# Gated mix of memory attention and GEGLU on one core: repeated waits on TensorE, and the last output part in partition halves

## The chip, the cores and the metric

The kernel runs on one core of a Trainium2 chip. The metric is the device time of one execution in microseconds, the median of three runs. One further execution is taken with the hardware profiler; every duration below that has a row is from that one execution.

## The reference

```python
x = A_x                                            # (1, 2048, 512) bf16
g = sigmoid((x * gate_w).sum(-1, keepdims=True))   # one gate per token
a = A_ref(x, wq, wk, wv, wo, beta)                 # attention with a memory
b = B_ref(x, w_gate, w_up, w_down)                 # (gelu(x@w_gate) * (x@w_up)) @ w_down, inner width 1792
return g * a + (1 - g) * b
```

`A_ref` splits the 2048 tokens into 4 segments of 512 and has 32 heads of width 16. In each segment it takes a causal softmax attention inside the segment, and adds, weighted by `sigmoid(beta)`, a read of a memory `M, z` that the earlier segments have built from `phi(k)` and `v`, with `phi(t) = t + 1` for positive `t` and `exp(t)` else. Then `M` and `z` take up the segment's own keys and values, and the joined heads go through `wo`.

## The kernel before

**The work of one segment.** Keys, queries and values are dense products (`K`, `Q`, `V`: four TensorE products of 128x512 each into one PSUM bank), each evicted by ScalarE or VectorE. The scores are "fills" (`st`): eight row-tiled products that fill the four banks of `psX`; ScalarE takes the exponential of all 2048 columns at once (`exp`, line 661) into `pt`, and GpSimd multiplies the causal triangles in (`msk`, line 667). There are 18 fills in a segment, 72 in all, and as there is only one `psX` a fill has to wait until the exponential of the fill before has been read out. `pv` (line 698) multiplies with the values: 64 small products in one go, four times a segment. VectorE transposes and normalizes (`tp`, `pvp`, `ot`). `mz` and `nd` write and read the memory. The GEGLU part has 14 gate products (`G`), 14 up products (`U`, one after the other `Us_fta` and `Us_ftb` of two TensorE products each, both into the same bank, line 487), 14 multiplications on VectorE (`h`, line 824), and the down products `out` (line 837). Behind them stand the output projection `wo` (line 854), the eviction of the down product with the factor 1-g (`wev`, lines 842 and 845), the sum of the two on VectorE (`oev`, line 858) and the store (`dma`, line 863).

**What sets the order.** The program is a list of tasks with reads and writes. `ORDER`, a text at the end of the file, names all of them in the order in which they are issued; a digit behind a colon is the PSUM bank or buffer taken, an `a` or `d` says whether ScalarE or VectorE does an eviction. Each engine gets its own tasks in this order. `Emitter.finalize` works out which semaphore values each instruction has to wait for, leaving out those that the engine has already waited for, and `Emitter.emit` (line 237) puts a `wait_ge` for each ahead of the instruction. The last of these waits rides on the instruction itself. Further ones become wait instructions of their own; in the trace they are `EVENT_SEMAPHORE` at line 241.

**The end of the program.** The fast program takes the exponentials without subtracting a row maximum. A test (`chk`, `okrow`, `oksum`, `flag`, lines 727 to 738) finds out whether that was safe for the data. Every engine loads the flag into a register (`reg_*`, `TENSOR_LOAD`, line 742), and compares and branches (line 961): when all is well it jumps to the end, past a second, general program of that engine that subtracts the maxima. That program is long: on VectorE 1024 of its instructions are the row maxima (two for each of 512, lines 770 to 774), on TensorE the fills have a second product for each of theirs. Near the start of its stream each engine executes a hint that names this branch (line 951; `HINT` says behind how many instructions). Behind the branch all engines drain and meet (line 971). SyncE, and only SyncE, waits for the stores: for the early ones ahead of its last three tasks, for two of them ahead of its branch, and for the last three behind it (line 992).

**The last two row blocks.** Token blocks 14 and 15 (128 tokens each) have their output projection and the sum in two column halves of 256, to shorten the last steps. Block 14 is stored as a whole from SyncE. Block 15 is stored in two parts: columns 0 to 255 from SyncE, columns 256 to 511 from ScalarE.

## Time and profile before

| | |
|---|---|
| median of 3 runs | 267.12 us (267.05 to 267.35) |
| the profiled execution's own time | 268.07 us |
| its span, first to last instruction | 266.3 us |
| around the span | 268.07 - 266.3 = 1.77 us |
| granted TensorE clock | 0.997 |
| TensorE busy | 254.0 us |
| VectorE, ScalarE, GpSimd busy | 214.5, 209.6, 96.6 us |

PE is the TensorE matmul, PEld its weight load, DVE VectorE, ACT ScalarE, POOL GpSimd, SP SyncE; a `q` behind the name (PEldq, SPq) marks an instruction of that engine's sequencer: waits, register loads, branches, drains and the issue of DMAs. `L487` is line 487 of the kernel. In a list of instructions by source line the columns are the engine, the operation, the count, the shortest, median and longest duration in ns, and the first and last start in us. In a list by time they are start, duration, engine, line, operation, and in brackets the idle time before with what ended it. The end of a TensorE product is modelled, about 380 ns for 128x512, while the next one can start 216 ns after it.

### The profile page before, as it was taken

The numbers are of one execution on the slowest core, as the hardware profiler recorded it, in microseconds if no ns is written. First come the engines' busy times: TensorE is split into PE (matmuls) and PEld (weight loads), VectorE is DVE, ScalarE is ACT, GpSimd is POOL, SyncE is SP. The second block draws the span as 40 slices with busy tenths as digits, with TensorE's granted clock in tenths as the row PEclk, the third lists the DMA queues.
The fourth block names the chain that finished last, engine by engine and source line by source line (L and its number), as shares of the span: only waits on it lengthen the run. The fifth ranks groups of instructions, "written<-read, shape, count | busy, mean of one in ns | idle before, by whom it ended". The sixth has DMA issues, their size and how long they took to land.

```text
span 266.3 us, 6561 instructions
## 1 busy us (share of the span) xinstructions
PE 254.0 (95%) x2729; PEld 112.4 (42%) x2766; DVE 214.5 (81%) x421; ACT 209.6 (79%) x174; POOL 96.6 (36%) x159
## 2 busy tenths in 40 slices
PE   7999999999999999999999999999999999999991
PEld 4634434444344444444434344334444443434450
DVE  0676776689999797999798989998988986959872
ACT  2578999989899999999988879568889976577420
POOL 6024332065551526160452644433407217263400
PEclk9999999999999999999999999999999999999998
DMA  6897179802547203002021001000110000000011
GB/s 205 237 177 234 39 108 192 245 23 62 158 62 100 61 20 109 12 0 63 0 64 42 20 2 62 2 21 2 43 35 7 0 2 21 21 22 1 22 39 47
DMA packets 26624, 17.19 MB, mean 65 GB/s; under 512 B 14302, under 2 KB 26078, under 8 KB 26590
## 3 DMA queue, kind: packets, MB, share of 16 engines
q1 hardware_dynamic: 26014, 16.27, 25.3%
q10 hardware_dynamic: 576, 0.46, 0.6%
q8 instruction: 22, 0.36, 0.6%
q14 instruction: 12, 0.10, 0.1%
HBM read 10.36 MB, written 2.10 MB: 47 GB/s over the span
## 4 chain that ended last, share of the span: by engine, by line
PE 93%; issue 2%; DMA 2%; DVE 1%; SPq 0%
PE psD L487 51%; PE psD L837 18%; PE psX L645 9%; PE psD L698 6%; PE psD L854 5%; DMA pt<-in_A_x_dram 2%; PE psD L582 1%; PE psD L515 1%; PE psX L600 0%; PE psD L509 0%; DVE ost L858 0%; SPq L357 0%; PE psD L588 0%; PE psX L908 0%; DVE kD L526 0%
## 5 line engine op out<-in xcount | busy, mean ns | idle before, releaser
L661 ACT ACTIVATE pt<-psX 128x2048 bf16<-128x2048 f32 x72 | 135.1, 1877 | 28.6 <-PE psX L645 27.4
L667 POOL TENSOR_TENSOR pt<-pt,ctri 128x256 bf16<-128x256 bf16 x128 | 91.2, 719 | 151.8 <-ACT pt L661 147.3
L487 PE MATMUL psD<-xT,wu 128*128 128x512 bf16 x214 | 54.1, 380 | 1.4 <-issue 1.3
L837 PE MATMUL psD<-wd,gb 128*128 128x512 bf16 x217 | 54.1, 380 | 0.9 <-issue 0.8
L487 PE MATMUL psD<-xT,wg 128*128 128x512 bf16 x217 | 54.1, 380 | 0.9 <-issue 0.8
L824 DVE TENSOR_TENSOR gb<-psD,gb 128x512 bf16<-128x512 f32 x56 | 37.3, 684 | 8.6 <-PE psD L487 8.3
L837 PEld LDWEIGHTS psD<-wd,gb 128*128 128x128 bf16 x224 | 20.5, 98 | 26.1 <-issue 2.8
L487 PEld LDWEIGHTS psD<-xT,wu 128*128 128x128 bf16 x224 | 20.3, 98 | 26.1 <-issue 2.8
L487 PEld LDWEIGHTS psD<-xT,wg 128*128 128x128 bf16 x224 | 20.1, 98 | 26.4 <-issue 3.2
L557 DVE STREAM_TRANSPOSE tT<-psD 128x512 f32<-128x512 f32 x35 | 24.1, 703 | 7.7 <-PE psD L698 5.8
L645 PE MATMUL psX<-qT,kD 32*128 32x192 bf16 (+7 forms) x512 | 28.5, 287 | 0.0
L645 PEld LDWEIGHTS psX<-qT,kD 32*128 32x128 bf16 x512 | 8.2, 92 | 25.2 <-ACT pt L661 20.9
L698 PE MATMUL psD<-pt,vnat 64*17 64x128 bf16 (+7 forms) x512 | 18.8, 283 | 0.0
L698 PE MATMUL psD<-pt,vsh 64*17 64x128 bf16 (+7 forms) x512 | 18.3, 283 | 0.0
L710 DVE SCALAR_TENSOR_TENSOR ob<-tT,gq,rcall 128x256 bf16<-128x256 f32 x32 | 16.6, 517 | 1.1
L487 PE MATMUL psD<-wv,xT 128*128 128x512 bf16 x61 | 16.8, 380 | 0.4 <-issue 0.3
L487 PE MATMUL psD<-xT,wq 128*128 128x512 bf16 x59 | 16.2, 379 | 0.7 <-issue 0.5
L480 DVE CAST gb<-psD 128x512 bf16<-128x512 f32 x19 | 12.9, 686 | 3.9 <-PE psD L487 3.9
L854 PE MATMUL psD<-wo,oT 128*128 128x512 bf16 (+1 forms) x69 | 15.5, 354 | 0.5 <-issue 0.5
L698 PEld LDWEIGHTS psD<-pt,vnat 64*17 64x17 bf16 x512 | 11.6, 86 | 8.9 <-POOL pt L667 4.2
L815 ACT ACTIVATE gb<-psD 128x512 bf16<-128x512 f32 x28 | 14.8, 603 | 0.6 <-PE psD L487 0.5
L842 ACT ACTIVATE wds<-psD,omgt 128x512 f32<-128x512 f32 x8 | 5.5, 686 | 12.1 <-PE psD L837 7.4
(99 smaller groups left out, 275.8 us busy)
## 6 DMA issues: line engine op xcount, KB each, us to landing
xg<-in_A_x_dram SPq DMA_DIRECT2D x16, 128.0 KB, 2.2
out_dram<-ost SPq DMA_DIRECT2D x15, 128.0 KB, 1.7
wg<-in_B_w_gate_dram SPq DMA_DIRECT2D x2, 896.0 KB, 6.8
wu<-in_B_w_up_dram SPq DMA_DIRECT2D x2, 896.0 KB, 5.9
wd<-in_B_w_down_dram SPq DMA_DIRECT2D x2, 896.0 KB, 6.7
vsh<-vnat SPq DMA_DIRECT2D x16, 68.0 KB, 2.1
wq<-in_A_wq_dram SPq DMA_DIRECT2D x2, 256.0 KB, 5.3
wv<-in_A_wv_dram SPq DMA_DIRECT2D x1, 512.0 KB, 3.9
```

What stands on the lines that cost most here:

```text
L480: (DVE, 0.60, [I(lambda e: e.tensor_copy(dst, src()), [bk(sl), *reads], writes)]),
L487: one(f"{name}{'abcd'[h // 2]}", PE, 2 * T_MM, [I(lambda e, i=i: e.matmul(BK[sl.i][:, :], lhs(i), rhs(i), start=(i == 0), stop=(i == n - 1 ...
L557: one(f"tp{name}", DVE, 0.605, [I(lambda e, ts=ts, bank=bank: e.transpose(tT[ts.i][:, :], bank()), [key], [("tT", ts)])])
L645: ins.append(I(lambda e, c=c, kb=kb, ncol=ncol, c0=c0, g=g: e.matmul(XALL[:, g * 512 + c0:g * 512 + c0 + ncol], kD[b][quad(g), c, kb, :], ...
L661: one(f"exp{s}_{name}", ACT, 2048 * 0.000833 + 0.05, [I(lambda e: e.activation(pt[slot][:, :, :], xin, ACTF.Exp, scale=ATT_SCALE), [("X", ...
L667: ins.append(I(lambda e, mv=mv: e.tensor_tensor(mv, mv, cm, ALU.mult), [("pt", slot), ("causal",)], [("pt", slot)]))
L698: ins.append(I(lambda e, kb=kb, slot=slot, c0=c0, n=n, g=g, c=c, r0=r0, sl=banks[j], va=va: e.matmul(BK[sl.i][32 * c:32 * c + 17, 64 * kb: ...
L710: I(lambda e, ts=ts, t=t, j=j, dst=dst, r=r: e.scalar_tensor_tensor(out=dst, in0=t_rows(ts, 16), scalar=gq[:, 2 * t + j:2 * t + j + 1], in ...
L815: one(f"gd{s}_{ft}", ACT, 0.485, [I(lambda e, gi=gi, f=f, sl=sl: e.activation(gb[gi][:, f, :], BK[sl.i][:, :], ACTF.Gelu_apprx_tanh), [bk( ...
L824: one(f"h{s}_{ft}", DVE, 0.605, [I(lambda e, sl=sl, gi=gi, f=f: e.tensor_tensor(gb[gi][:, f, :], BK[sl.i][:, :], gb[gi][:, f, :], ALU.mult ...
L837: mm.append(I(lambda e, fb=fb, gi=gi, f=f, q=q, sl=sl: e.matmul(BK[sl.i][:, :], gb[gi][:, f, q], wd[:, fb, :], start=(fb == 0), stop=(fb = ...
L854: one(f"wo{s}_{qt}_{ci}", PE, 4 * T_MM / len(parts), [I(lambda e, kb=kb, q=q, so=so, c=c: e.matmul(BK[so.i][:, c], oT[:, kb, q], wo[:, kb, ...
```

## The change

Three edits go together. The first makes `emit` put the last wait that the engine had met a further `again` times ahead of an instruction, and sets `again = 2` for the last instruction of every `U` task: the second and the fourth product of each of the 56 up products, 112 instructions on TensorE. Each of them then has two more waits, both for a value that has been reached.

The second changes the stores of block 15. Columns 0 to 255 go out from ScalarE. Columns 256 to 511 go out in two DMAs, partitions 0 to 63 from SyncE and 64 to 127 from ScalarE. The lists of stores that SyncE waits for move by one.

The third is a new `ORDER`: the same tasks, and the one new store, in another order, with some evictions given to the other engine and other banks.

```diff
         self.inc = False
+        self.again = 0
...
         self.order = []
+        self.met = {}
...
             for sem, val in spec.waits:
                 e.wait_ge(sem, val)
+                self.met[eng] = sem, val
+            for _ in range(spec.again):
+                e.wait_ge(*self.met[eng])
             ins = spec.fn(e)
...
-                        one(f"dma{gt}_{ci}", (SP, ACT)[last and ci], 0.5, [I(lambda e, gt=gt, oi=oi, d=d: e.dma_start(
-                            out[0, gt * 128:(gt + 1) * 128, d], ost[oi][:, d]), kd, [("out", gt, ci)],
-                            dma_sem=sem(f"s_out{gt}_{ci}"))], lat=2.0)
-                        outs.append(f"s_out{gt}_{ci}")
+                        rows = ((ci, SP if not last else ACT, 0, P),) if not (last and ci) else ((1, SP, 0, 64), (2, ACT, 64, P))
+                        for n, eng, lo, hi in rows:
+                            one(f"dma{gt}_{n}", eng, 0.5, [I(lambda e, gt=gt, oi=oi, d=d, lo=lo, hi=hi: e.dma_start(
+                                out[0, gt * 128 + lo:gt * 128 + hi, d], ost[oi][lo:hi, d]), kd, [("out", gt, n)],
+                                dma_sem=sem(f"s_out{gt}_{n}"))], lat=2.0)
+                            outs.append(f"s_out{gt}_{n}")
...
+    for t, eng, instrs in order:
+        if t.name[0] == "U":
+            instrs[-1].again = 2
     em.finalize()
...
-            for name in outs[:-5]:
+            for name in outs[:-6]:
...
-            for name in outs[-5:-3]:
+            for name in outs[-6:-4]:
...
-            for name in outs[-3:]:
+            for name in outs[-4:]:
...
 ORDER = """
-ld_x0_0 wake0:0 ld_x0_1 ld_wk0 ident wake1 ld_wk1 xtr0_00 ld_x0_2 xtr0_01 ld_x0_3 ld_wk2 ld_wq0 xev0_00:a xev0_01:a
...
-wo3_0_0:3 wev3_1:a wo3_1_0:0 oev3_0_0 dma11_0 oev3_1_0 out3_3_2 out3_3_3 chk3 out3_3_4 dma12_0 okrow wev3_2:a
-wo3_2_0:2 wev3_3:a wo3_2_1:3 oev3_2_0 wo3_3_0:0 wo3_3_1:1 oev3_2_1 dma13_0 oev3_3_0 oev3_3_1 oksum:2 dma14_1 dma15_0
-flag dma15_1 reg_pe reg_act reg_dve reg_pool reg_sp
+ld_x0_0 causal1 wake0:0 ident ld_x0_1 ld_wk0 wake1 ld_wk1 xtr0_00 ld_x0_2 xtr0_01 ld_x0_3 ld_wk2 xtr0_03 xev0_00:a
+xev0_01:d xev0_03:d ld_wq0 xtr0_02 ld_wq1 xev0_02:d K0_k0:1032 ld_wv K0_k1 xtr0_11 xtr0_10 ld_beta ld_wg0 xtr0_12
...
+G1_3a:2 mzm0 G1_3b G1_4a:3 Gev1_2:a gs4 msk0_3D gs5 st1_0A:0 G1_4b exp1_0A phkb1_2 msk1_0A U0_12a:1 Gev1_3:d ld_xg6
+ld_xg7 U0_12b Kev2_1:d Gev1_4:d h0_12 pv0_3:20 st1_0B:0 tp0_d30:1 pvp0_30 ld_wd1 out0_1_0:1 ld_x3_3 pvp0_21 out0_1_1
+tp0_d31:2 out0_1_2 exp1_0B K2_3a:2 st1_0D:0 phqb1_0 phkc1_2 K2_3b out0_1_3 K2_2a:0 Q2_3a:3 gs6 exp1_0D K2_2b ktr1_0
+Kev2_3:a Q2_3b ktr1_1 Kev2_2:a vsh1_01 ot0_2 msk1_0B Qev2_3:a st1_0E:0 phqc1_2 ktr1_2 msk1_0D K2_0a:2 V2_3a:0 V2_3b
+Vev2_3:d exp1_0E K2_0b out0_0_0:3 st1_0C:0 Kev2_0:a out0_0_1 pvp0_31 exp1_0C kpada2_3 vsh1_00 ld_wo20 out0_3_0:0 gs7
...
+ot3_3 wo3_0_0:0 wo3_1_0:3 oev3_0_0 oev3_1_0 chk3 out3_3_2 out3_3_3 dma12_0 out3_3_4 okrow wev3_2:a dma13_0 wo3_2_0:3
+oev3_2_0 wo3_2_1:0 wo3_3_0:2 oev3_2_1 wev3_3:a wo3_3_1:3 oksum:1 oev3_3_0 oev3_3_1 flag dma14_1 dma15_0 dma15_1
+dma15_2 reg_pe reg_act reg_dve reg_pool reg_sp
```

Counted in the two texts: TensorE has 524 tasks in both, and 78 stretches of row-tiled work (fills, `pv`, `mz`, `nd` and the first transposes) between dense products in both. In both, exactly ten dense products of 128x512 lie between one fill and the next in 33 places. The first 16 DMAs that SyncE issues are the same in the same order. The last five tasks of TensorE, and the last five of VectorE, come in the same order in both.

## Prediction

> **What bounds the kernel now.** I read the page first, then TensorE's waits, then the last microseconds line by line.

> ```profile
> span 266.3 us, 6561 instructions
> ...
> PE 254.0 (95%) x2729; PEld 112.4 (42%) x2766; DVE 214.5 (81%) x421; ACT 209.6 (79%) x174; POOL 96.6 (36%) x159
> ```

> TensorE is busy for 95% of the span. That its products also follow each other without holes is in a stretch of the timeline, which I chose because a wait instruction stands in it (below):

> ```profile
> 47.97 1.89 PE L487 MATMUL psD<-xT,wg 128*128 128x512 bf16 x8
> 49.70 1.03 PE L487 MATMUL psD<-xT,wq 128*128 128x512 bf16 x4
> 50.56 0.81 PE L487 MATMUL psD<-xT,wu 128*128 128x512 bf16 x3
> ```

> From 47.97 to 50.56 twelve products start in 2.59 us, 0.216 us each. The list of TensorE's own waits has nothing longer than 0.8 us, and its largest entry is small:

> ```profile
> PE psD L487 <- issue: 3.2, 20, 0.2
> PE psX L399 <- PEq L1112: 0.8, 1, 0.8
> ```

> So until about 260 us the time is the number of products and of changes between dense and row-tiled work, and another order can save there only by having fewer. Then comes the end. The chain of waits for the last 16 us runs over TensorE, the last sums and the flag, and stops at 261.01; the span stops at 266.3. What lies between are sequencer instructions, seen by listing the branch line and the drain line:

> ```profile
> 260.04 0.92 DVE ost L858 x2
> 260.96 0.05 DVE flag L738
> ```

> ```profile
> L961 POOLq COMPARE_BRANCH  x1: 65/65/65, 261.6 to 261.6; - x1
> L961 PEldq COMPARE_BRANCH  x1: 4322/4322/4322, 261.6 to 261.6; - x1
> L961 SPq COMPARE_BRANCH  x1: 83/83/83, 261.6 to 261.6; - x1
> L961 DVEq COMPARE_BRANCH  x1: 84/84/84, 261.8 to 261.8; - x1
> L961 ACTq COMPARE_BRANCH  x1: 68/68/68, 261.9 to 261.9; - x1
> ```

> ```profile
> L971 SPq DRAIN  x1: 13/13/13, 262.9 to 262.9; - x1
> L971 PEldq DRAIN  x1: 63/63/63, 266.0 to 266.0; - x1
> ```

> ```profile
> L992 SPq EVENT_SEMAPHORE  x1: 27/27/27, 262.6 to 262.6; - x1
> ```

> **This is the fact on which I build:** five engines take the same branch, four need 65 to 84 ns, TensorE 4322. Its drain stands at 266.0, the next latest, SyncE's behind the last store, at 262.9. TensorE's branch alone holds the kernel open for the last 3.1 us, and the stores are hidden behind it.

> **The change part by part.**

> *The waits.* 56 up products have two halves each: 112 instructions get two waits. As before, one rides on the instruction and one stands alone, so TensorE's stream is 112 instructions longer. What a standing wait costs:

> ```profile
> L241 PEldq EVENT_SEMAPHORE  x1: 51/51/51, 48.8 to 48.8; - x1
> ```

> ```profile
> L241 PEldq EVENT_SEMAPHORE  x3: 51/51/51, 28.0 to 28.2; - x3
> ```

> Bare, it is 112 x 0.051 = 5.7 us of the sequencer's time. The first row is the wait inside the stretch quoted above, where the products keep their 0.216 us: the sequencer runs ahead of the array. The second row gives its pace: three waits, each with a few products behind it, start within 0.2 us, so about 0.1 us each, against 2 x 0.216 = 0.43 us that the two products of a half take. Queued behind such a wait are the half's second product and all that follows, and for these wait `h` and then `out`; none is late as long as the lead lasts. Bounds 0 to +5.7 us; I take 0, the nearest row being a wait among dense products. The cover is the lead; without it the full 5.7 us come due.

> *What the waits move.* They are the only part of the change that acts on the branch: the branch and its target now lie 112 places further on in TensorE's stream. No row shows what makes the branch slow. Distance alone does not: VectorE's branch also jumps over more than 1024 instructions of the general program and takes 84 ns. Being hinted does not tell them apart either:

> ```profile
> L951 PEldq BRANCH_PREFETCH_HINT  x1: 50/50/50, 0.9 to 0.9; - x1
> ...
> L951 DVEq BRANCH_PREFETCH_HINT  x1: 51/51/51, 4.8 to 4.8; - x1
> ```

> Two differences are left: the length of the stream between hint and branch (2729 products and 2766 loads against 421 instructions), and the place at which the branch falls in it. The change leaves the first and shifts the second. If place decides, the branch falls to what the other four show; if length decides, nothing moves. Bounds for the branch: 0.07 us to 4.3 us, or a little over. I take the low end, because four rows of five lie there and a delay that strikes one long stream at one spot looks to me more like an unlucky place than a law; this is the choice in this forecast, and the trace does not force it.

> Then SyncE's drain is last. From TensorE's end (266.0 + 0.06) to SyncE's (262.9 + 0.01) it is 3.15 us; the meeting behind it (266.06 to 266.3) stays. TensorE's branch starts at 261.6 and may take up to 1.3 us before it is last again. **Term: -3.15 us.**

> [...]

> *The stores.* With the branch gone they are on the path. Now:

> ```profile
> L863 SPq DMA_DIRECT2D out_dram<-ost x16: 332/340/747, 90.1 to 260.6; - x16
> L863 ACTq DMA_DIRECT2D out_dram<-ost x1: 367/367/367, 261.0 to 261.0; - x1
> ```

> ```profile
> out_dram<-ost SPq DMA_DIRECT2D x15, 128.0 KB, 1.7
> ...
> out_dram<-ost ACTq DMA_DIRECT2D x1, 64.0 KB, 1.6
> ```

> The last sum ends at 260.96, the last store is issued at 261.0 and lands 1.6 us later, 262.6, where SyncE's last wait ends. A store of 128 KB takes 1.7 us and one of 64 KB 1.6: half the size saves 0.1. Two halves of 32 KB should save between 0 and 0.2; I take 0.05. On ScalarE the neighbour's issue (0.37 us from some 260.5, when the first of the two sums is done) is over by 260.9, just ahead of its second store. SyncE's part is issued at 261.0 and its register load, which was at 261.0, goes behind it by about 0.37 us: load 0.50, branch 0.08, so 262.0, still ahead of 262.6. **Term: -0.05 us;** with the slow branch, 0.

> *The order.* The numbers of TensorE tasks (524) and row-tiled stretches (78) are equal, so its work is too. At the start:

> ```profile
> 1.24 0.29 POOL L425 TENSOR_SCALAR_AFFINE_SELECT ident<-ident 128x128 bf16<-128x128 bf16 x1 [0.23 <-POOL ident L424]
> 1.48 0.15 POOL L416 MEMSET ctri<- 128x64 bf16 x1
> 1.70 0.24 POOL L417 TENSOR_SCALAR_AFFINE_SELECT ctri<-ctri 128x64 bf16<-128x64 bf16 x1
> ```

> ```profile
> 6.45 0.77 PE L908 MATMUL psX<-ident,pt 128*128 128x128 bf16 x8 [0.38 <-DMA pt<-in_A_x_dram]
> ```

> `causal1` goes ahead of `ident` on GpSimd: about 0.4 us, `ident` ready by some 2.0 us instead of 1.5. The transposes that need it are held by the load of x, whose second half lets them go at 6.45; those DMAs keep their places in SyncE's queue. Cost 0.

> The one spot that I worked out is where the gaps differ: 13 and 11 products between the fills 1_0D, 1_0E and 1_0C, with three ScalarE evictions before the exponential of 1_0E.

> ```profile
> 81.00 1.88 ACT L661 ACTIVATE pt<-psX 128x2048 bf16<-128x2048 f32 x1
> 82.82 0.60 ACT L479 ACTIVATE kT<-psD 128x512 bf16<-128x512 f32 x1
> 83.31 1.05 ACT L499 ACTIVATE phq<-phq 128x1024 bf16<-128x1024 bf16 x1
> 84.26 1.87 ACT L661 ACTIVATE pt<-psX 128x2048 bf16<-128x2048 f32 x1
> ```

> ```profile
> 35.23 0.40 PE L645 MATMUL psX<-qT,kD 32*128 32x320 bf16 x8
> ...
> 35.68 1.88 ACT L661 ACTIVATE pt<-psX 128x2048 bf16<-128x2048 f32 x1 [0.18 <-PE psX L645]
> ```

> ScalarE's starts follow at 1.82, 0.49 and 0.95 us, and an exponential starts 0.45 us behind its fill. With 1_0B at 0: exponential 0.45, `phqb` 2.27, free 3.22; 1_0D at 2.59, its exponential 3.22, three evictions from 5.04, free 6.51; 1_0E at 2.59 + 0.43 + 13 x 0.216 = 5.83, its exponential 6.51 to 8.39; 1_0C at 5.83 + 0.43 + 11 x 0.216 = 8.64. It clears by 0.25 us. If ScalarE took each full duration instead of its pace, the exponential would end at 8.94 and the fill come 0.4 us late. I take 0, bound +0.4.

> **Sum** for the profiled execution: 266.3 - 3.15 - 0.05 = 263.1 us of span. The median lies 267.12 - 266.3 = 0.8 above this span (the profiled execution's own 268.07 lies 1.8 above); keeping that offset, 263.9 us.

> **The rivals.**

> *The branch stays slow* because the stream's length decides. For it: TensorE alone has the long stream. Against it: the hint reaches its branch 257 us later on VectorE. The stores remain hidden; 267.1 us, up to 267.5 with the late fill.

> [...]

> *The waits show* (the other side). Place: the 112 halves, above all behind long row-tiled stretches, where many small products pass quickly and the lead may be spent. Price 0.051 us each, 5.7 in all: 269.6 us even with the branch freed. It decides once more than 3.2/0.051 = 63 of the 112 stand open. Against it is the unbroken stretch at 48.8; with the 0.1 us pace the lead grows by 0.3 us at each half.

> **How the numbers follow.** A measurement of this kernel can tell about 0.2%, 0.5 us, from no change. Branch freed 0.55 (263.9; its own range 263.3, with the full 0.2 from the stores and some luck, to 264.5 with the late fill); in part 0.08; stays slow 0.25, of which 0.20 within 0.2% and 0.05 beyond it by more than one late fill; waits show 0.12. Faster 0.55 + 0.08 = 0.63, same 0.20, slower 0.05 + 0.12 = 0.17. The range goes from 263.3 to 267.6, the slow branch with its late fill included; outside are the open waits and the tails, under 2 in 10.

> **What would show it.** Right: TensorE's branch at line 961 well under 1.3 us, the last drain SyncE's, the span ending 0.4 us behind the last store; 112 more waits at line 241 on TensorE and dense products still 0.216 us apart. Wrong: that branch at about 4.3 us again, with the stores' change unseen; or up products spaced wider than 0.216 us where the waits stand; or a fill behind ScalarE at 1_0C.

## The result and the profile after

The changed kernel takes 266.24 us (median of 22 runs, 264.80 to 269.32), the kernel before, timed beside it, 267.09 us (22 runs). The ratio is 0.9953, 95% interval 0.9933 to 0.9974. A second set of runs of the same kernel gave 0.9953 (0.9924 to 0.9982). So the change makes the kernel faster, but by 0.5% where 1.2% were forecast: 266.24 us against 263.9.

Three of the 22 runs were slow executions (268.79 to 269.32 us, granted clock 0.993 and 0.994) and are left out from here on. The other 19, with a median of 265.58 us, fall into two groups, ten from 264.8 to 265.6 us and nine from 266.2 to 267.4. The profiled execution (265.39 us, span 263.7) belongs to the lower group; the profiled execution of before (268.07) lies above the median of its kernel. The two profiles are therefore 2.6 us apart, the medians 0.85, and both numbers have to be explained.

First the branch, listed by its line as in the prediction (line 971 is the old 961, line 981 the old 971):

```profile
L971 POOLq COMPARE_BRANCH  x1: 65/65/65, 261.8 to 261.8; - x1
L971 DVEq COMPARE_BRANCH  x1: 84/84/84, 261.8 to 261.8; - x1
L971 PEldq COMPARE_BRANCH  x1: 390/390/390, 261.8 to 261.8; - x1
L971 SPq COMPARE_BRANCH  x1: 83/83/83, 262.6 to 262.6; - x1
L971 ACTq COMPARE_BRANCH  x1: 76/76/76, 262.7 to 262.7; - x1
```

TensorE's branch has gone from 4322 to 390 ns. The drains and SyncE's last waits (line 1002, the old 992) show what is last now:

```profile
L981 PEldq DRAIN  x1: 110/110/110, 262.3 to 262.3; - x1
...
L981 SPq DRAIN  x1: 13/13/13, 263.4 to 263.4; - x1
```

```profile
L1002 SPq EVENT_SEMAPHORE  x2: 17/22/28, 263.1 to 263.2; - x2
```

TensorE drains at 262.3 instead of 266.0, and SyncE's drain behind the stores is the last, as forecast. But it stands at 263.4, not at 262.9 or a little before. The stores take longer to land than before, seen in the list of DMA issues from 256 us on (KB each, median us from issue to landing):

```profile
out_dram<-ost SPq DMA_DIRECT2D x3, 128.0 KB, 1.7
out_dram<-ost ACTq DMA_DIRECT2D x1, 64.0 KB, 1.6
out_dram<-ost SPq DMA_DIRECT2D x1, 32.0 KB, 1.9
out_dram<-ost ACTq DMA_DIRECT2D x1, 32.0 KB, 2.1
```

A half of 32 KB lands after 1.9 and 2.1 us, the whole 64 KB part took 1.6. The engines that issue the two halves also load the flag later and more slowly, which the rows of the flag's register load show, first of the changed kernel, then of before:

```profile
L747 SPq TENSOR_LOAD <-flag x1: 810/810/810, 261.6 to 261.6; - x1
L747 ACTq TENSOR_LOAD <-flag x1: 967/967/967, 261.7 to 261.7; - x1
```

```profile
L742 SPq TENSOR_LOAD <-flag x1: 502/502/502, 261.0 to 261.0; - x1
...
L742 ACTq TENSOR_LOAD <-flag x1: 474/474/474, 261.4 to 261.4; - x1
```

What ends last of all this is the landing: both halves are issued at 261.1 us, the later one lands 2.1 us on, at 263.2, and there SyncE's last wait ends. The slower loads are over before: ScalarE, the later of the two engines, branches at 262.7.

The repeated waits are where they were meant to be, and the products beside them keep their pace:

```profile
L246 PEldq EVENT_SEMAPHORE  x112: 51/51/51, 49.7 to 244.1; - x112
```

```profile
50.34 0.38 PE L492 MATMUL psD<-xT,wq 128*128 128x512 bf16 x1
50.55 1.03 PE L492 MATMUL psD<-xT,wu 128*128 128x512 bf16 x4
51.42 0.59 PE L492 MATMUL psD<-xT,wg 128*128 128x512 bf16 x2
51.85 0.38 PE L492 MATMUL psD<-xT,wu 128*128 128x512 bf16 x1
```

From 50.34 to 51.85 seven products start in 1.51 us, 0.216 each. Comparing each wait's start with the start of the product that it precedes, the sequencer runs 0.08 to 1.9 us ahead of the array; it never falls behind.

Last, the traffic of instructions. In the lists of DMA queues by window (packets, MB, share of 16 engines) the queue `q8 instruction` carries packets of 16 KB, 22 in the span of before (0.36 MB). TensorE's stream there has 5573 instructions up to the branch, about 253 for each packet by this estimate; the places in the experiments below put a block at 256. Before, from 262 to 265 us:

```profile
q8 instruction: 1, 0.02, 3.9%
```

The same view of the changed kernel, from 250 to 261.5 us, a window in which before has none:

```profile
q8 instruction: 1, 0.02, 0.5%
```

The trace dates these packets. Before, one starts at 247.36 and the next at 262.55 (it takes 1.88 us), 0.95 us behind the start of the branch. I read that one as the block of the branch's target, fetched only when the branch is taken. In the changed kernel one starts at 252.11, ten us ahead of the branch, and none while the branch lasts (261.81 to 262.20). This gave theory P: whether the target's block comes early depends on the place of the branch among blocks of 256 instructions, and the 112 waits move it. The rivals: it was the new order or the stores, or any lengthening does it.

### The profile page after: what moved, and what is told of

Same layout as the page of the kernel before. It is cut to its first block, busy times and chain, and to the rows that moved or that the text cites. A ratio compares the mean times of both kernels' runs of the same rounds, so it can differ in the third digit from the quotient of the medians.

```text
span 263.7 us, 6671 instructions
## 1 busy us (share of the span) xinstructions
PE 253.8 (96%) x2729; PEld 112.5 (43%) x2766; DVE 215.3 (82%) x419; ACT 210.7 (80%) x176; POOL 100.4 (38%) x159
## 4 chain that ended last, share of the span: by engine, by line
PE 93%; issue 2%; DMA 2%; DVE 1%; SPq 0%; DVEq 0%
PE psD L492 52%; PE psD L842 19%; PE psX L650 9%; PE psD L703 7%; PE psD L859 5%; DMA pt<-in_A_x_dram 2%; PE psD L520 1%; DVE gb L829 0%; PE psD L587 0%; PE psX L605 0%; PE psD L514 0%; DVE ost L863 0%; SPq L362 0%; DVE tT L562 0%; PE psX L915 0%
## 5 line engine op out<-in xcount | busy, mean ns | idle before, releaser
L672 POOL TENSOR_TENSOR pt<-pt,ctri 128x256 bf16<-128x256 bf16 x128 | 95.0, 749 | 148.1 <-ACT pt L666 143.6
L492 PE MATMUL psD<-xT,wu 128*128 128x512 bf16 x216 | 55.3, 380 | 1.2 <-issue 1.1
L847 ACT ACTIVATE wds<-psD,omgt 128x512 f32<-128x512 f32 x10 | 6.9, 686 | 13.0 <-PE psD L842 7.9
L492 PE MATMUL psD<-wv,xT 128*128 128x512 bf16 x61 | 16.1, 380 | 0.5 <-issue 0.5
L485 DVE CAST gb<-psD 128x512 bf16<-128x512 f32 x19 | 12.8, 682 | 3.5 <-PE psD L492 3.1
## 6 DMA issues: line engine op xcount, KB each, us to landing
xg<-in_A_x_dram SPq DMA_DIRECT2D x16, 128.0 KB, 2.4
out_dram<-ost SPq DMA_DIRECT2D x15, 128.0 KB, 1.7
```

Source lines behind the costliest of these rows:

```text
L485: (DVE, 0.60, [I(lambda e: e.tensor_copy(dst, src()), [bk(sl), *reads], writes)]),
L492: one(f"{name}{'abcd'[h // 2]}", PE, 2 * T_MM, [I(lambda e, i=i: e.matmul(BK[sl.i][:, :], lhs(i), rhs(i), start=(i == 0), stop=(i == n - 1 ...
L672: ins.append(I(lambda e, mv=mv: e.tensor_tensor(mv, mv, cm, ALU.mult), [("pt", slot), ("causal",)], [("pt", slot)]))
```

## The experiments

All medians are in us, and all ratios are to the kernel before, timed beside the run, with their 95% interval. "Place" counts TensorE's fast stream: a product as two instructions (the page of before has 2766 weight loads and 2729 products), a standing wait as one. That the packets follow this count is read from the places in e1, e2, e4 and e5 below. The branch of before stands at 5573 and that of the changed kernel at 5680: the 112 waits move it on, and the new order, which needs five other standing waits fewer, moves it back by 5.

### The three edits apart: e1_waits_only and e2_no_waits

The first is the kernel before with the first edit alone:

```diff
+            for _ in range(spec.again):
+                e.wait_ge(*self.met[eng])
...
+        if t.name[0] == "U":
+            instrs[-1].again = 2
```

> The kernel before with nothing changed but the 112 repeated waits. Theory P (place): TensorE's branch is slow only at certain places of its stream, because there the instruction block that it jumps to is fetched only at the branch (one 16 KB packet right behind it, 262.55 us before, against a packet at 252.11, ten us ahead of it, after). The waits move it 112 places; so the branch takes at most 0.5 us, TensorE's drain comes ahead of SyncE's at 262.9, the span is 263.1 to 263.3 and the ratio to the kernel before 0.988 to 0.995, as good as the whole change or better. Rival O (order and stores): the branch was freed by the new order or the new stores; then it takes about 4.3 us again and the ratio is 0.998 to 1.002. Rival W (the waits cost): ratio above 1.002 with the dense products wider than 0.216 us apart.

The second is the changed kernel without it:

```diff
-            instrs[-1].again = 2
+            instrs[-1].again = 0
```

> The changed kernel without the 112 repeated waits: new order and new stores alone; TensorE's stream is some 8 instructions shorter than before. Theory P (place): branch back at 3 to 4.5 us, the last packet of its instruction queue behind the branch, none in the 10 us ahead of it; ratio 0.997 to 1.003, the stores hidden. Rival O (order and stores): branch at 0.4 us as in the changed kernel, ratio 0.993 to 0.997. If the order costs or saves something of its own, the start of the branch differs from 261.6 to 261.8 us by that much.

Measured: e1 265.66, ratio 0.9944 (0.9922 to 0.9965); e2 269.06, ratio 1.0087 (1.0053 to 1.0120). The branch in e1, then in e2:

```profile
L969 PEldq COMPARE_BRANCH  x1: 385/385/385, 262.0 to 262.0; - x1
```

```profile
L971 PEldq COMPARE_BRANCH  x1: 4317/4317/4317, 262.6 to 262.6; - x1
```

The waits free the branch, order and stores don't: theory P and "any lengthening" stand, the rival of order and stores is out. The totals fit less well: e1's ratio lies at the slow end of its range and its span, 263.5 us, above the 263.1 to 263.3 expected, and e2 is slower by more than either theory allowed. The start of each product against the kernel before (e1) and the changed kernel (e2) shows one jump, near 94 us. There `pv1_0` (64 small products) is followed at once by `mz1` (68). TensorE's timeline in e1 (start, duration, engine, line, operation; in brackets the idle time before):

```profile
92.66 0.58 PE L587 MATMUL psD<-vnat,phkt 128*32 128x34 bf16 x45
94.29 0.30 PE L587 MATMUL psD<-vnat,phkt 128*32 128x34 bf16 x18 [1.06 <-issue]
```

and in e2:

```profile
92.87 0.73 PE L587 MATMUL psD<-vnat,phkt 128*32 128x34 bf16 x60
94.93 0.20 PE L587 MATMUL psD<-vnat,phkt 128*32 128x34 bf16 x4 [1.33 <-issue]
```

TensorE stands still in the middle of one task, after 45 products in one kernel and 60 in the other, with nothing to wait for ("issue"). Neither profile that I had compared before shows such a stretch.

### Where the branch is slow: e3_shift256, e4_minus10 and e5_plus28

e3 is the kernel before with repeated waits ahead of the second half of every up and gate product and of 16 of the key and query products, 256 more instructions on TensorE:

```diff
+        if t.name[0] in "UG" and t.name[1] in "0123" or t.name[0] == "K" and t.name[1] in "123" or t.name[:2] == "Q1":
+            instrs[-1].again = 2
```

> [...] Theory P (place): place counts modulo 256, so the branch is slow again, 3 to 4.5 us, ratio 0.998 to 1.003, though more than twice as many waits were added as in the change. Rival N (any longer stream frees the branch): 0.1 to 0.5 us, ratio 0.988 to 0.995. Rival W (the waits cost, 0.05 us each): up to 12.8 us more, ratio up to 1.048.

For e4 the start loses five products on constants, which no output uses:

```diff
-        for i, cols in enumerate(([512] * 5 + [128] * 3, [128] * 1)):
+        for i, cols in enumerate(([512] * 3 + [128] * 0, [128] * 1)):
```

> The kernel before with 3 in place of 8 of the products on constants at the start, which no output uses: TensorE's stream is 10 instructions shorter, with no wait added. Theory P (place): the branch stays on the slow side (the kernel before lies some tens of instructions below the place from which the target is fetched early, and this one 10 further below): 3 to 4.5 us, ratio 0.998 to 1.003. If the edge lies just below the kernel before instead, the branch takes at most 0.5 us and the ratio is 0.988 to 0.995. [...]

```diff
+        if t.name[:2] == "U3":
+            instrs[-1].again = 2
```

> The kernel before with the repeated waits on the up products of the last segment alone: 28 more instructions on TensorE, all behind 200 us. By the runs so far (branch 385 to 390 ns with 10 fewer or 112 more instructions than before, 3.6 to 4.3 us with 0, 5 fewer or 256 more) the slow zone begins 5 to 10 places ahead of the place of before; this run looks for its other end. Theory P (the target is fetched as soon as TensorE enters the block of 256 that holds the branch): entry is now some 33 to 38 instructions ahead of the branch, at about 258.3 us; a fetch that needs 3.3 us from its trigger (the branch of before with a packet of 0.9 us) is done by 261.6, so the branch takes 0.1 to 1.0 us and the ratio is 0.988 to 0.995. Rival (the fetch is triggered further inside the block): 3.3 to 4.3 us, ratio 0.998 to 1.002. In either case no idle stretch at 94 us, as nothing ahead of it has moved.

Measured: e3 267.24, ratio 1.0018 (0.9998 to 1.0038); e4 266.19, ratio 0.9976 (0.9952 to 1.0000); e5 265.14, ratio 0.9937 (0.9912 to 0.9963). Their branches, in this order:

```profile
L969 PEldq COMPARE_BRANCH  x1: 3617/3617/3617, 260.9 to 260.9; - x1
```

```profile
L961 PEldq COMPARE_BRANCH  x1: 385/385/385, 263.1 to 263.1; - x1
```

```profile
L969 PEldq COMPARE_BRANCH  x1: 473/473/473, 261.7 to 261.7; - x1
```

256 more instructions, with more than twice the waits of the change, leave the branch slow; 10 fewer or 28 more free it. So it is not length and not the waits, but the place modulo 256, and 256 more waits cost nothing that can be seen (267.24 us with the slow branch, ratio 1.0018). For e4 I had expected the slow side first and named the other as the alternative: the edge lies just ahead of the place of before. Its ratio is spoilt by two things. The second eight products of line 509 start 0.18 us apart instead of 0.11, which puts it 0.5 us behind the kernel before at 8.6 us; and the stretch at 94 us is there again, now behind all 64 products. In e5, where I had expected none, it comes behind 59:

```profile
93.90 0.78 PE L582 MATMUL psD<-vnat,phkt 128*32 128x34 bf16 x64
95.50 0.39 PE L588 MATMUL psD<-phq,zq 128*8 128x512 bf16 x4 [0.82 <-issue]
```

```profile
92.85 0.72 PE L587 MATMUL psD<-vnat,phkt 128*32 128x34 bf16 x59
94.15 0.20 PE L587 MATMUL psD<-vnat,phkt 128*32 128x34 bf16 x5 [0.57 <-issue]
```

Here the two observations meet. `mz1` begins at place 1892 in e1, 1862 in e2, 1854 in e4 and 1864 in e5. Adding two for each product done ahead of the stretch gives 1892 + 90, 1862 + 120, 1854 + 128 and 1864 + 118: 1982 in all four. I read that as the end of a block. Fourteen blocks of 256 on, at 1982 + 14 x 256 = 5566, lies the edge at the branch, which stands at 5573 before, 5568 in e2, 5829 (7 behind the next edge, 5822) in e3: slow (4322, 4317 and 3617 ns). It stands at 5563 in e4 (253 behind the edge ahead), 5601 in e5, 5680 after: fast (385, 473 and 390 ns). Fourteen and 256 have a measure of their own: in the trace of before the packets at 88.26 and 247.36 us are fourteen apart (15 in the window from 88 to 248), and if they belong to the two edges, the second of which lies between 5563 (fast) and 5568 (slow), a block has between 255.8 and 256.1 instructions. So the branch is slow 2 and 7 instructions behind an edge and fast at 35, 114 and 253 (e5, after, e4); what lies between was not tried. Branch and target move together in all these kernels. That it is the branch's place which counts is read from the early packet, which follows the edge: it starts at 252.2 us in e1, where the product at 5566 starts at 251.5, and at 256.8 in e5, where that product starts at 258.4.

### Stores, spread and place: e6_old_stores, e7_after_again and e8_late112

e6 is the changed kernel with the old stores:

```diff
-                        rows = ((ci, SP if not last else ACT, 0, P),) if not (last and ci) else ((1, SP, 0, 64), (2, ACT, 64, P))
...
+                        one(f"dma{gt}_{ci}", (SP, ACT)[last and ci], 0.5, [I(lambda e, gt=gt, oi=oi, d=d: e.dma_start(
+                            out[0, gt * 128:(gt + 1) * 128, d], ost[oi][:, d]), kd, [("out", gt, ci)],
...
-oev3_2_0 wo3_2_1:0 wo3_3_0:2 oev3_2_1 wev3_3:a wo3_3_1:3 oksum:1 oev3_3_0 oev3_3_1 flag dma14_1 dma15_0 dma15_1
-dma15_2 reg_pe reg_act reg_dve reg_pool reg_sp
+oev3_2_0 wo3_2_1:0 wo3_3_0:2 oev3_2_1 wev3_3:a wo3_3_1:3 oksum:1 oev3_3_0 oev3_3_1 dma14_1 dma15_0
+flag dma15_1 reg_pe reg_act reg_dve reg_pool reg_sp
```

> The changed kernel with the stores of before (block 15 in two column halves, the first from SyncE, the second from ScalarE): new order and repeated waits alone. Theory S (the partition halves cost): from the flag copy to the end of the span 2.2 us, as in the kernel with the repeated waits alone (261.25 to 263.47), in place of 2.7 us in the changed kernel (260.94 to 263.66); ratio to the changed kernel's 0.9953 lower by 0.002, about 0.993. Rival (the stores are hidden or as good): 2.7 us, ratio 0.995 or more. Branch 0.4 us in both.

e7 is the changed kernel again, without an edit.

> The changed kernel once more, unchanged, for a second profile. Its runs lie at spans of 263.1 to 263.9 and at 264.5 to 265.0, and its first profile was of the lower kind. Theory F (fetch stall): in some executions TensorE stands still for 0.8 to 1.3 us at 94 us, in the 264 small instructions of pv1_0 and mz1, as three of four experiments did, because its next instruction block has not come; then a profile with a span of 264.5 or more shows that stall, one of 263.1 to 263.9 doesn't. Rival (start): the spread comes from the first 8 us (loads of x and the clock), and the two profiles differ there. Ratio 0.9935 to 0.9975.

```diff
+        if t.name[0] == "U" and t.name[1] in "123":
+            instrs[-1].again = 4 if t.name[1] == "3" else 2
```

> The kernel before with the same 112 further instructions on TensorE as in the change, but none of them ahead of 94 us: repeated waits on the up products of segments 1 and 2, twice as many on those of segment 3. Old order, old stores. Theory F (fetch stalls, two places): branch at 0.4 us as with the repeated waits alone, and no idle stretch at 94 us, since the block boundaries there lie as in the kernel before; span 262.4 to 263.2, ratio 0.988 to 0.992, better than the changed kernel. Rival (the stretch at 94 us comes by chance, not by place): ratio 0.994 as with the repeated waits alone.

Measured: e6 265.44, ratio 0.9946 (0.9922 to 0.9971); e7 265.43, ratio 0.9953 (0.9924 to 0.9982); e8 265.33, ratio 0.9939 (0.9919 to 0.9958). In e6 the tail from the start of the flag's copy (262.59) to the end of the span (264.80) takes 2.2 us as theory S said, but the medians of e6 and e7 do not tell the stores' cost, because the stretch at 94 us covers it. e6 has the order and the waits of the changed kernel, and its profile (266.54 us, one of the five of its twelve runs above 265.9) shows what the changed kernel's profile did not:

```profile
93.81 0.64 PE L587 MATMUL psD<-vnat,phkt 128*32 128x34 bf16 x46
95.68 0.28 PE L587 MATMUL psD<-vnat,phkt 128*32 128x34 bf16 x17 [1.24 <-issue]
```

`mz1` begins at 1890 there: 1890 + 92 = 1982 once more. This speaks for the upper group of the changed kernel's runs being the group with this stretch; no execution of that group was profiled, and e12 below tests it. The profile of e7 (granted clock 0.993) shows the longest stretch, behind 46 products too:

```profile
93.51 0.63 PE L587 MATMUL psD<-vnat,phkt 128*32 128x34 bf16 x46
96.15 0.28 PE L587 MATMUL psD<-vnat,phkt 128*32 128x34 bf16 x17 [2.00 <-issue]
```

The rival of e7's expectation, the start, fails: the first product of line 520 starts at 8.08 us here and at 8.05 in the first profile (across the kernels it differs more, from 7.32 us in e1 to 8.37 in e6, so single profiles also differ by their starts). But the stretch costs more than its own length here. Right behind it the granted clock is at half, as three windows show (window, its length, busy time of TensorE, its weight loads, VectorE, ScalarE and GpSimd, granted clock, DMA share, GB/s):

```profile
90.00:96.30 6.30, 4.30 (x146) 2.36 (x144) 4.82 (x10) 4.45 (x4) 0.67 (x1) 1.00 0.46 61
96.40:99.70 3.30, 3.30 (x25) 1.02 (x15) 1.64 (x4) 2.26 (x2) 0.31 (x1) 0.50 0.03 7
99.80:103.00 3.20, 3.20 (x22) 1.31 (x21) 2.81 (x5) 2.01 (x2) 0.93 (x2) 1.00 0.01 3
```

Half the clock (0.50) for some 3.4 us is 1.7 us of work, an estimate from these windows; with the 2.0 us of the stretch that makes up the 3.7 us by which this span (267.4 us) exceeds that of the first profile (263.7). That standing still lowers the clock is not shown by one trace.

My expectation of e8 fell: its stretch is there (0.57 us, behind 59 products), although `mz1` lies exactly as in the kernel before. Its stream, like that of e5, is that of before up to there, so that place is not free of the stretch; the profiled execution of before merely escaped. The packet of the block that begins at 1982 tells the executions apart: it started at 87.8 to 90.2 us in the four profiles so far without a stretch in which the edge at 1726 lies close ahead of `pv1_0` (before, after, and e10 and e11 below), and at 91.7 to 93.4 in the seven that show one. What makes it late stays open. It is not only when the array passes 1726: the product there starts at 88.1 us in e1 and at 88.5 in e10, but the packet at 91.9 in the one and at 87.9 in the other. In the seven the packet comes behind the issue of the next load of `xT` (89.7 to 92.5 us), in the four ahead of it; whether that load holds it up was not tested.

### The edge moved away from the small products: e9_early

```diff
+    for t, eng, instrs in order:
+        if t.name == "mz1":
+            break
+        if t.name[0] in "UG" and t.name[1] in "0123" or t.name[0] == "K" and t.name[1] in "123" or t.name[:2] == "Q1":
+            instrs[-1].again = 2
```

> The kernel before with repeated waits on TensorE only ahead of mz1 (up, gate and some key and query products up to 93 us): 104 instructions more, none behind 94 us; old order, old stores. Theory F: a block of 256 instructions ends at one fixed count of TensorE's stream, whatever the kernel; the idle stretch at 94 us came after 45, 46, 59, 60 and 64 products of mz1 as the streams were shifted, which is one and the same count (1982), 14 blocks ahead of the edge of the slow branch (5566). With 104 more the edge at 1726 lies 112 instructions ahead of pv1_0 in dense work instead of 8 ahead of it, so the block that ends in mz1 is asked for some 6 us earlier: no idle stretch at 94 us in any execution; the branch lies 111 behind its edge, 0.4 us. Span 262.4 to 263.1, ratio 0.988 to 0.992, spread under 1.2 us. Rival (the stretch is a matter of the small products or of DMA traffic): a stretch of 0.6 to 1.3 us again, ratio 0.994.

Measured: 264.71, ratio 0.9885 (0.9849 to 0.9921), six runs from 264.50 to 265.05. Branch and `mz1`:

```profile
L971 PEldq COMPARE_BRANCH  x1: 385/385/385, 261.6 to 261.6; - x1
```

```profile
93.41 0.78 PE L587 MATMUL psD<-vnat,phkt 128*32 128x34 bf16 x64
94.02 0.40 PE L593 MATMUL psD<-phq,zq 128*8 128x512 bf16 x4
```

As theory F said, with a spread of 0.55 us in six runs against 2.6 in the changed kernel's 19. The edge at 1982 still lies inside `mz1` (which begins at 1968); what has moved away from the small products is the edge ahead of it, 1726, and the packet of the block of 1982 now starts at 82.2 us. In e3, and in e12 and e13 below, it starts at 81.6 to 82.5, and their profiles have no stretch either.

Since e3 has the same waits up to `mz1` and the same free passage there, but the slow branch, e3 and e9 differ by the branch alone: 267.24 - 264.71 = 2.5 us. The two ran in different sets, beside which the kernel before took 267.00 and 267.89 us. Free of that is the time from the start of the flag's copy to the end of the span, within one trace and with the old stores: 5.4 us before, 4.7, 4.8 and 4.7 in e3, e10 and e11 (slow branch), 2.2 in e1, e4, e5, e6, e8 and e9. So the slow branch costs 2.5 to 2.6 us in three executions and 3.2 in that of before.

### The hint: e10_late_hint and e11_no_hint

Both start from e1, whose branch takes 0.385 us.

```diff
-        em.emit(eng, slice(p.start, p.start + HINT[eng]))
+        at = p.stop - 14 if eng == PE else p.start + HINT[eng]
+        em.emit(eng, slice(p.start, at))
```

> The kernel before with the 112 repeated waits (branch at 0.39 us) and TensorE's prefetch hint moved from the 6th step of its stream to some 28 instructions ahead of the branch, some 90 behind the edge of the branch's block. Theory H1 (the hint must stand when the branch's block is entered; then the target is fetched in place of the next block): branch 3.3 to 4.3 us, ratio 0.999 to 1.002. Theory H2 (the hint itself sets off the fetch): asked for at about 259 us and 3 us ahead of the branch, so 0.4 to 0.7 us, ratio 0.994.

```diff
-        e.br_eq(regs[eng], GOOD, on_true=done, on_false=general).branch_hint(ahead)
+        br = e.br_eq(regs[eng], GOOD, on_true=done, on_false=general)
+        if eng != PE:
+            br.branch_hint(ahead)
```

> The kernel before with the 112 repeated waits and no prefetch hint on TensorE (the other engines keep theirs). Theory H (the hint is what lets the target's block come ahead of the branch): branch 3.3 to 4.3 us wherever it lies, ratio 0.999 to 1.002. Rival (the hint does nothing; the place alone decides): 0.4 us, ratio 0.994.

Measured: e10 267.25, ratio 0.9993 (0.9961 to 1.0025); e11 267.81, ratio 1.0002 (0.9978 to 1.0026). The branches:

```profile
L970 PEldq COMPARE_BRANCH  x1: 3697/3697/3697, 261.2 to 261.2; - x1
```

```profile
L969 PEldq COMPARE_BRANCH  x1: 3589/3589/3589, 261.1 to 261.1; - x1
```

Theories H1 and H hold. In both a packet still comes at 251.6 us, which I take to be when the branch's block is entered, but the one that I read as the target's comes only at the branch (262.2 and 262.1), although the hint of e10 was executed at 257.3 us, 3.9 us ahead of it. So in e10 the hint brought no packet by itself. My reading, from the packets of e1 (252.2 us, branch 385 ns) against these two: a hint that stands when the branch's block is entered makes the target the next block to be fetched.

How the entry sets off that fetch is not settled. In the three slow kernels with an early hint (before, e2, e3) the target's packet starts 0.95 to 1.12 us behind the start of the branch, as it does in e10 and e11 (1.01 us). Yet in before the product at place 5566 had started 1.7 us ahead of the branch (259.94 against 261.60 us). So with 2 or 7 instructions between edge and branch the packet was not a little late: in these three it did not start before the branch did.

### Order and stores without the two stalls: e12_early_after and e13_early_order

The edit of e9 in place of the repeated waits, in the changed kernel (e12) and in e6, the changed kernel with the old stores (e13):

```diff
     for t, eng, instrs in order:
-        if t.name[0] == "U":
+        if t.name == "mz1":
+            break
+        if t.name[0] in "UG" and t.name[1] in "0123" or t.name[0] == "K" and t.name[1] in "123" or t.name[:2] == "Q1":
             instrs[-1].again = 2
```

> The changed kernel (its order, its stores) with its 112 repeated waits replaced by repeated waits ahead of mz1 only, as in the last experiment but one: TensorE's stream 8 instructions shorter than the changed kernel's, the edge at 1726 now 109 instructions ahead of pv1_0, the branch 106 behind its edge. Theory F+S (two fetch waits, and stores that cost 0.3 to 0.5 us): no idle stretch at 94 us, branch at 0.4 us, from the flag's copy to the end 2.7 us; median 264.7 + 0.3 to 0.5 = 265.0 to 265.2 us, spread under 1.2 us in place of 264.8 to 267.4, ratio 0.989 to 0.992. Rival (the new order has a cost of its own besides): over 265.4 us, or a spread as wide as the changed kernel's.

> The same with the stores of before: the new order alone, its two fetch waits taken away. Theory F+S: as the old order with early waits, 264.6 to 264.9 us, from the flag's copy to the end 2.2 us, and 0.3 to 0.5 us under the run with the new stores. Rival O (the order has a cost or a gain of its own): more than 0.4 us away from 264.7 us, with the place where TensorE falls behind seen against the old order.

Measured: e12 265.18 (264.84 to 265.54, 12 runs), ratio 0.9929 (0.9904 to 0.9953); e13 264.55 (264.39 to 264.81, 8 runs), ratio 0.9897 (0.9861 to 0.9933). The page's first line and the flag's copy, of e12 and of e13:

```profile
span 263.6 us, 6700 instructions
```

```profile
L743 DVE COPY flag<-psD x1: 134/134/134, 260.9 to 260.9; 1x1 f32<-1x1 f32 x1
```

```profile
span 262.7 us, 6698 instructions
```

```profile
L743 DVE COPY flag<-psD x1: 135/135/135, 260.5 to 260.5; 1x1 f32<-1x1 f32 x1
```

From the flag to the end it is 2.7 us with the new stores and 2.2 with the old. That is 0.5 us for the new stores within the traces; by the medians they cost 265.18 - 264.55 = 0.63 us, somewhat more than expected. The new order on its own costs nothing that can be seen (264.55 against 264.71 in e9, ratios 0.9897 and 0.9885). The lower group of the changed kernel's runs (264.8 to 265.6) is e12's range; its upper group is that plus the stretch at 94 us, and e12, which shows no stretch, has no such group in its 12 runs. With that the accounts close roughly, and both e9 and e13 are faster than either of the two kernels.

## Why the prediction was right and wrong, step by step

**The fact on which it was built** was right. TensorE's branch was last by 3 us, the shift freed it, and behind it SyncE's drain is last. "An unlucky place" rather than a law of long streams was the right choice: e3 rules out length. But it was a choice that, in its own words, "the trace does not force", made without a mechanism, and so in part luck: that the branch is slow 2 or 7 instructions behind an edge, and also without a hint (3589 ns in e11) or with a late one (3697 in e10), is nowhere in it. For the chance of 0.08 of a branch freed in part there was no row; with the change it took 390 ns. Two details were off at no cost. The branch fell to 390 ns and not to the other engines' 65 to 84, where up to 1.3 us were free; and the waits are not the only part that moves it, as the order shifts it too (by 5, in e2).

**"Term: -3.15 us"** was mis-sized. It was read from one execution in which the packet at the branch took 1.88 us; that packet took 1.15 us in e3 (branch 3617 ns). e3 against e9 gives 2.5 us for the branch, between medians, and so do the ends of the traces of e3, e10 and e11. The prediction had noted that the profiled execution lay 0.95 us above the median and kept an offset, but did not ask which of its own terms that execution had inflated.

**"Two halves of 32 KB should save between 0 and 0.2; I take 0.05"** is the step that failed outright, in its sign. The halves cost 0.63 us (e12 against e13; 0.5 within the traces). The bound came from 128 KB at 1.7 and 64 KB at 1.6 us, that is, from size alone; but the halves landed after 1.9 and 2.1 us, and that landing is what SyncE waits for last. Why they land later stays open: two DMAs were issued in the same moment from two engines (issues of 542 and 562 ns in place of 367), and no run separates size, the moment and the two engines. The loads of 810 and 967 ns behind them are over before the landing.

**The waits at 0** were right: dense products at 0.216 us beside them, and e3 and e9 add 256 and 104 without a cost that can be seen.

**The order at 0** was right for its work (e13 against e9). The changes between dense and row-tiled work, equal in number, have their price in the trace of before: the fill at 32.63 us starts 0.31 behind the dense product ahead of it, and the next dense one 0.33 behind the fill, where dense products follow each other at 0.216. The fill 1_0C, its one bound, comes on time: it starts at 83.84 us, 2.81 behind 1_0E and 0.28 behind the end of the exponential, where 0.25 was forecast (its late case is 8.94 - 8.64 = 0.3 us by its own sum, not 0.4). But the forecast had no term for what order and shift do at 94 us. In part of its executions, nine of the 19 by the groups, the changed kernel stands still there; 1.24 us were measured in e6. The prediction asked for the branch alone what its place does, and did not look for other places where small products pass quickly: the 264 instructions of `pv1_0` and `mz1` pass in about 1.7 us in the kernel before, while 2.4 us lie between the start of the packet and the next product in e5.

Summed up against before: 2.5 saved, 0.6 given back by the stores, and about 1.2 given back in about half of the executions. From 267.1 that gives 265.2 for the lower group and 266.4 for the upper, whose means are 265.2 and 266.7; the mean of the 19 runs is 265.9, and 266.24 is the median of all 22. The sum takes the kernel before as free of the stretch; how many of its executions have it, no run tells.

## What to carry to other kernels

When an engine's branch or a burst of small instructions stalls with nothing to wait for, look at the engine's instruction packets in the DMA view, count instructions, and test with a shift of 256 against a smaller one, as e3 against e4 and e5: here only the smaller ones freed the branch, so it was the place and not the work. Cheap filler ahead of the spot can then move both edges at once, as e9 did with 104 waits (264.71 us). Hold a term that comes from one execution against the spread of its kernel, and price a split DMA by when its parts land, which need not follow their bytes (32 KB after 1.9 and 2.1 us here, 64 KB after 1.6).
